# Local attention and two mixture layers on one core: copies ahead of exponentials on ScalarE, and one conversion operation on GpSimd

## The chip, the core and the metric

The kernel runs on one core of a Trainium2 chip. A core has five engines with queues of their own, each worked off in order: TensorE (PE in the rows, PEld for its weight loads), VectorE (DVE), ScalarE (ACT), GpSimd (POOL), and SyncE (SP), which here only starts transfers. They wait for each other through semaphores. The metric is the device time of one execution in microseconds (us). Lower is better.

## The reference

```
scores = scale * q @ k.T                    # 4 batches x 8 heads, 576 x 576, head width 64
mask   = (0 <= rel < 64), else -1e9         # each row looks back at most 63 positions
attn   = exp(scores - rowmax) / (rowsum + 1e-9);   x = attn @ v        # 2304 x 512
h = x @ w_in;  g = elu(h);  x = g @ w_out   # 512 -> 2048 -> 512
P = exp(x @ w_gate - max);  8 rounds of: divide rows by their sums, columns by theirs
out = sum over 8 experts e of  P[:, e] * (relu(x @ w1[e]) @ w2[e])     # 512 -> 1024 -> 512
```

The inputs q, k, v are 32-bit; `w_in` and `w_out` come as pairs of 32-bit words of 64-bit numbers.

## The kernel before

The program is one stream of calls in a fixed order, and each engine executes its own instructions in the order of these calls. Nothing is reordered at run time.

**Attention.** The 4 x 8 heads are 16 pairs of heads, each cut into three groups of 192 rows, so there are 48 groups, `n` = 0 to 47, group 0 to 2 for the first pair and so on. The loop `for m in range(NST + 3)` takes two groups a step through a pipeline of five stages, each a step apart. In step `m` the names are `nxt` (groups that are transposed), `new` (scores), `mid` (exponentials), `old` (probabilities transposed) and `fin` (multiplied by v):

- `pair_T` (L308, L314): four transposes on TensorE into `ptr`, then one ScalarE copy into `qkT`.
- `grp_S` (L340, L349): twelve score matmuls into `s`, then on VectorE three reductions, which add the mask, write `sp` and take the row's minimum into `smx`.
- `grp_E` (L366): three exponentials on ScalarE, in place on `sp`, with the row sums into `smx`.
- `grp_N` (L377, L378, L381): for both groups of a step, two short VectorE operations on `smx`, then on GpSimd one multiplication of `sp` for each group.
- `grp_P` (L389, L391): three transposes on TensorE into `pt`, then a ScalarE copy into `pT`.
- `v_shift` (L294): two GpSimd copies that build `ve`, the values shifted by 64 rows, once for each pair, in the step in which the pair's first group is in `old`.
- `grp_V` (L404) multiplies `pT` by `ve` and `vo`, and `grp_XH`, `grp_X` (L432, L439) write the result as a high part (ScalarE) and a low part (VectorE).

**Weights.** `f64_parts` turns a block of 64-bit weights into 32-bit ones, in six operations: L152 and L155 on VectorE (from the high words to `t`), L158 (the low words scaled, in place), L161 on ScalarE (magnitude of the high words), then L162 and L163 on VectorE, which join the parts. L179 and L180 on GpSimd (`w_split`) make a high and a low part from `t`. There are 32 blocks. The calls wait in a list `bg`, and `run_bg` takes two of them at three places of an attention step from step 1 on: ahead of `pair_T` and after each of the two halves of the step. A block takes eight calls (six operations, the next load, the split). Blocks 0 to 7 go through steps 1 to 11, two more are converted in steps 13 to 16. Blocks 10 to 15 run in the drain after the attention, the others in the middle stage.

**After that.** `slot` puts the matmuls of the first mixture layer between those of the attention, from step 9 on; before step 7 it puts a matmul on zeros (`warm`, L1170) there. After the last step the rest of the first part of that layer is drained; then come the other three parts of the layer (the middle stage), the gate, and the eight experts, which take most of the time.

Of the kernel before, what the change touches and what calls it, by code (L numbers as in the profile page):

```python
# [11 lines left out]
AF = mybir.ActivationFunctionType  # L12
ALU = mybir.AluOpType
# [5 lines left out]
def kernel(  # L19
# [14 lines left out]
    nc = tc.nc  # L34
# [13 lines left out]
    scale = 1.0 / float(D) ** 0.5  # L48
# [59 lines left out]
    def ps_ac(name):  # L108
        return ps.tile([P, 512], F32, tag="ac", bufs=4, name=name)
# [16 lines left out]
    def w_load(k):  # L126
        if k >= 2 * UF * NU:
            return
        u, i, m = w_at(k)
        f0 = (u * UF + i) * P  # L130
        t = raw_p.tile([P, 2 * DM], I32, tag="raw", bufs=NRAW, name="raw")
        if m == 0:
            nc.sync.dma_start(
                out=t.rearrange("p (c f) -> p c f", c=NCC),
                in_=w_in[:, 2 * f0:2 * (f0 + P)].rearrange("(c p) f -> p c f", p=P),
            )
        else:
            nc.sync.dma_start(out=t, in_=w_out[f0:f0 + P, :])
        raws[k] = t
# [3 lines left out]
    def f64_parts(src, t):  # L143

        w = src.rearrange("p (n two) -> p n two", two=2)
        lo, hi = w[:, :, 0], w[:, :, 1]
        ti = t.bitcast(I32)
        v = nc.vector  # L150
        return [
            lambda: v.tensor_scalar(  # L152
                ti, hi, 3, 0x3FFFFFF8, op0=ALU.logical_shift_left, op1=ALU.bitwise_and
            ),
            lambda: v.scalar_tensor_tensor(  # L155
                ti, hi, -0x40000000, ti, op0=ALU.bitwise_and, op1=ALU.bitwise_or
            ),
            lambda: nc.scalar.activation(  # L158
                lo, lo.bitcast(mybir.dt.uint32), AF.Copy, scale=2.0 ** -29
            ),  # L160
            lambda: nc.scalar.activation(hi.bitcast(F32), hi.bitcast(F32), AF.Abs),  # L161
            lambda: v.tensor_tensor(out=ti, in0=ti, in1=lo, op=ALU.add),  # L162
            lambda: v.scalar_tensor_tensor(  # L163
                t, hi.bitcast(F32), TINY, t, op0=ALU.is_ge, op1=ALU.mult
            ),
        ]
# [20 lines left out]
    def run_bg(n):  # L187
        for _ in range(min(n, len(bg))):
            bg.pop(0)()

    def w_tasks(k):
        def conv():
            bg[0:0] = w_conv(k) + [lambda: w_load(k + NRAW)]
            bg.pop(0)()

        return [conv, lambda: w_split(k)]
# [19 lines left out]
    def run_later():  # L216
        fs, later[:] = list(later), []
        for f in fs:
            f()
# [51 lines left out]
    def v_load(pi):  # L271
        b, hp = divmod(pi, NPAIR)
        h0 = 2 * hp

        vo = at.tile([P, 5, 2, D], F32, tag="vo", bufs=2, name="vo")
        for h in range(2):
            nc.sync.dma_start(
                out=vo[:, 0:4, h, :],
                in_=v[b, h0 + h, 0:512, :].rearrange("(w p) d -> p w d", p=P),
            )  # L280
        nc.sync.dma_start(
            out=vo[0:WIN, 4], in_=v[b, h0:h0 + 2, 512:S, :].rearrange("h p d -> p h d")
        )
        v_nat[pi] = (None, vo)
# [76 lines left out]
    def grp_E(n):  # L361
        sp, sm = g_st[n]
        g = n % NG
        for l in range(GRP):
            lo = WIN if g == 0 and l == 0 else 0
            nc.scalar.activation(  # L366
                sp[:, l, lo:],
                sp[:, l, lo:],
                AF.Exp,
                bias=sm[:, 0, l:l + 1],  # L370
                scale=-1.0,
                accum_out=sm[:, 1, l:l + 1],
            )

    def grp_N(ns):
        w = g_sm.pop(ns[0])[:, 1]
        nc.vector.tensor_scalar(w, w, 1e-9, None, op0=ALU.add)  # L377
        nc.vector.reciprocal(w, w)  # L378
        for i, n in enumerate(ns):
            sp, _ = g_st[n]  # L380
            nc.gpsimd.tensor_tensor(  # L381
                out=sp, in0=sp, in1=w[:, i].unsqueeze(2).to_broadcast([P, GRP, P]), op=ALU.mult
            )
# [10 lines left out]
    def grp_V(n, pv):  # L394
        pi, g = divmod(n, NG)
        b, hp = divmod(pi, NPAIR)
        pT = g_st.pop(n)
        ve, vo = v_nat[pi]
        for l in range(GRP):
            c = g * GRP + l  # L400
            vt, w = (vo, (c - 1) // 2) if c % 2 else (ve, c // 2)
            ks = slice(WIN, P) if c == 0 else slice(0, P)
            for h in range(2):
                nc.tensor.matmul(  # L404
                    pv[D * h:D * h + D, WIN * l:WIN * l + WIN],
                    vt[ks, w, h, :],
                    pT[ks, P * l + WIN * h:P * l + WIN * h + WIN],
                    start=True,
                    stop=True,
                )  # L410

    def grp_XH(ns, pv):
        segs = []
        for i, n in enumerate(ns):
            pi, g = divmod(n, NG)
            b, hp = divmod(pi, NPAIR)
            t0 = b * S + g * GRP * WIN
            t1 = t0 + GRP * WIN
            o = i * GRP * WIN
            while t0 < t1:  # L420
                j = t0 // TB
                n1 = min(t1, blocks[j][0] + blocks[j][1])
                x, z = t0 - blocks[j][0], n1 - blocks[j][0]
                if segs and segs[-1][:2] == [j, hp] and segs[-1][3] == x:
                    segs[-1][3] = z
                else:
                    segs.append([j, hp, x, z, o])
                o += z - x
                t0 = n1
        for j, hp, x, z, o in segs:  # L430
            src = pv[:, o:o + z - x]
            nc.scalar.activation(Xh[j][:, hp, x:z], src, AF.Copy)  # L432
            subs_x.append((j, hp, x, z, src))
# [3 lines left out]
    def grp_X():  # L437
        for j, hp, a, z, src in subs_x:
            nc.vector.tensor_tensor(  # L439
                out=Xl[j][:, hp, a:z], in0=src, in1=r(Xh[j][:, hp, a:z]), op=ALU.subtract  # L440
            )
        subs_x.clear()
# [703 lines left out]
    with tc.manual_schedule():  # L1146
# [43 lines left out]
        def ready():  # L1190
            if not avail:
                return False
            kind, _, x, h = avail[0]
            need = [(0, x, 0)] if kind == "i" else [(0, i, 1) for i in (2 * h, 2 * h + 1)]
            return all(w in wts for w in need)
# [14 lines left out]
        for m in range(NST + 3):  # L1210
            two = lambda x: [n for n in (2 * x, 2 * x + 1) if 0 <= n < NGRP]
            nxt, new, mid, old, fin = [two(m + 1 - x) for x in range(5)]
            if m == 0:
                for kk in range(NRAW):
                    w_load(kk)
            if ready():
                budget += 16.0 / per_b
            if fin:
                pv = ps_ac("pv")
                for i, n in enumerate(fin):  # L1220
                    grp_V(n, pv[:, i * GRP * WIN:(i + 1) * GRP * WIN])
                grp_XH(fin, pv)
            for n in new:
                grp_S(n)
            for n in mid[:1]:
                grp_E(n)
            for n in mid:
                if n and n % NG == 0:
                    v_load(n // NG)
            grp_X()  # L1230
            if fin and (m - 2) % per_b == 0:
                avail += subs[(m - 2) // per_b - 1]
            if m == 13:
                bg += [w_tasks(2 * UF + x)[0] for x in range(2)]
            rate = (2, 2, 2) if m else (0, 0, 0)
            run_bg(rate[0])
            slot(m, 2)
            for i in range(2):
                for n in nxt[i:i + 1]:
                    pair_T(n)  # L1240
                for n in old[i:i + 1]:
                    grp_P(n)
                for n in mid[1 - i:2 - 2 * i]:
                    grp_E(n)
                if i == 0:
                    for n in old:
                        if n % NG == 0:
                            v_shift(n // NG, 0)
                            v_shift(n // NG, 1)
                run_bg(rate[i + 1])  # L1250
                slot(m, 1 - i)
            if mid:
                grp_N(mid)
            run_later()
            for n in new:
                if n % NG == 0 and n // NG + 2 < B * NPAIR:
                    pair_load(n // NG + 2)
# [35 lines left out]
        for s, st in enumerate(steps):  # L1293
            u, j, i = st
# [50 lines left out]
        for u in range(1, 2 * KP):  # L1345
            n = 5 if 0 <= u - 2 < len(others) - N1 - N3 else 4
# [127 lines left out]
```

## Time and profile before

| what | value |
|---|---|
| median of 3 runs | 2026.53 us (2026.0 to 2027.12) |
| profiled execution, its own time | 2024.01 us |
| span of the profiled execution | 2022.2 us |
| TensorE busy | 1988.8 us (98%) |
| VectorE busy | 1412.7 us (70%) |
| ScalarE busy | 873.0 us (43%) |
| GpSimd busy | 772.4 us (38%) |
| mean granted TensorE clock | 0.995 |

The busy times are means over stages that differ. The 39 us of span in which TensorE has nothing lie mostly in the first 63 us and at the very end. A row of a profile names engine, line, output and inputs of an instruction, its start and its time in us; a trailing bracket gives the idle time of the engine ahead of it and what ended that.

### The profile page before, as it was taken

The numbers are of one execution on the slowest core, as the hardware profiler recorded it, in microseconds if no ns is written. First come the engines' busy times: TensorE is split into PE (matmuls) and PEld (weight loads), VectorE is DVE, ScalarE is ACT, GpSimd is POOL, SyncE is SP. The second block draws the span as 40 slices with busy tenths as digits, with TensorE's granted clock in tenths as the row PEclk, the third lists the DMA queues.
The fourth block names the chain that finished last, engine by engine and source line by source line (L and its number), as shares of the span: only waits on it lengthen the run. The fifth ranks groups of instructions, "written<-read, shape, count | busy, mean of one in ns | idle before, by whom it ended". The sixth has DMA issues, their size and how long they took to land.

```text
span 2022.2 us, 36406 instructions
## 1 busy us (share of the span) xinstructions
PE 1988.8 (98%) x13197; PEld 1849.8 (91%) x13197; DVE 1412.7 (70%) x2727; ACT 873.0 (43%) x1839; POOL 772.4 (38%) x753
## 2 busy tenths in 40 slices
PE   7999999999999999999999999999999999999998
PEld 6788888888878888889999999999999999999998
DVE  5754786858588665557777777777777777777776
ACT  6876455546443343333343333333334333333332
POOL 4533232324255555343353323233335333323332
PEclk9999999999999999999999999999999999999999
DMA  7540245438599999958878777777788877777774
GB/s 169 123 107 24 75 157 171 151 125 301 202 368 325 372 374 361 340 208 274 280 246 277 248 248 249 248 248 248 250 279 262 266 248 250 248 248 249 248 248 131
DMA packets 288628, 477.48 MB, mean 236 GB/s; under 512 B 78081, under 2 KB 144705, under 8 KB 284609
## 3 DMA queue, kind: packets, MB, share of 16 engines
q1 hardware_dynamic: 288368, 475.11, 71.7%
q8 instruction: 106, 1.74, 0.4%
q14 instruction: 74, 0.60, 0.1%
q10 hardware_dynamic: 80, 0.03, 0.0%
HBM read 348.14 MB, written 126.88 MB: 235 GB/s over the span
## 4 chain that ended last, share of the span: by engine, by line
PE 84%; DVE 5%; issue 4%; ACT 2%; DMA 2%; POOL 1%; SPq 1%; DVEq 0%; POOLq 0%; ACTq 0%
PE la L1043 15%; PE ob L1116 13%; PE oa L1116 13%; PE lb L1043 11%; PE ac L875 2%; PE ac L876 2%; PE ac L877 2%; PE p L857 2%; PE p L859 2%; PE p L858 2%; PE p L204 2%; PE p L205 2%; PE p L206 2%; PE ac L525 2%; PE ac L523 2%
## 5 line engine op out<-in xcount | busy, mean ns | idle before, releaser
L1025 POOL TENSOR_TENSOR h<-s,h 128x384 fp32r<-128x384 f32 x304 | 373.3, 1247 | 711.9 <-ACT h L1016 640.7
L1043 PE MATMUL la<-xf,w1f 128*128 128x384 f32 x1824 | 361.6, 336 | 6.5 <-ACT a L1056 4.8
L1043 PEld LDWEIGHTS la<-xf,w1f 128*128 128x128 f32 x1824 | 311.9, 189 | 8.7 <-ACT a L1056 5.2
L1116 PE MATMUL oa<-w2f,h 128*128 128x256 f32 x2394 | 307.3, 282 | 0.8 <-DVE acc L1137 0.8
L1116 PE MATMUL ob<-w2f,h 128*128 128x256 f32 x2394 | 307.3, 282 | 0.0
L1116 PEld LDWEIGHTS oa<-w2f,h 128*128 128x128 f32 x2394 | 302.0, 190 | 1.0 <-DVE acc L1137 1.0
L1116 PEld LDWEIGHTS ob<-w2f,h 128*128 128x128 f32 x2394 | 302.1, 190 | 0.0
L1021 DVE SCALAR_TENSOR_TENSOR h<-c,h 128x384 fp32r<-128x384 f32 x228 | 211.3, 927 | 120.0 <-ACT h L1016 119.9
L1043 PE MATMUL lb<-xf,w1f 128*128 128x384 f32 x1368 | 274.4, 335 | 0.0
L1043 PEld LDWEIGHTS lb<-xf,w1f 128*128 128x128 f32 x1368 | 237.5, 189 | 0.0
L1016 ACT ACTIVATE h<-s 128x384 fp32r<-128x384 f32 x304 | 154.7, 524 | 146.8 <-DVE s L1060 61.2
L1016 ACT ACTIVATE h<-c 128x384 fp32r<-128x384 f32 x228 | 119.1, 522 | 182.5 <-DVE c L1051 126.1
L1137 DVE SCALAR_TENSOR_TENSOR acc<-oa,Pr,acc 128x256 f32<-128x256 f32 x393 | 165.1, 474 | 42.2 <-PE oa L1116 42.2
L1137 DVE SCALAR_TENSOR_TENSOR acc<-ob,Pr,acc 128x256 f32<-128x256 f32 x381 | 160.1, 474 | 40.2 <-PE ob L1116 40.2
L696 POOL TENSOR_TENSOR sw<-rw 128x256 f32<-128x256 f32 x110 | 103.9, 944 | 214.6 <-DVE f L726 148.6
L1056 ACT ACTIVATE v<-la 128x384 f32<-128x384 f32 x76 | 37.4, 492 | 199.1 <-PE la L1043 199.0
L246 ACT ACTIVATE hh<-p 128x512 fp32r<-128x512 f32 (+1 forms) x80 | 39.2, 490 | 193.8 <-PE p L859 193.8
L857 PE MATMUL p<-xh,f 128*128 128x512 f32 (+1 forms) x320 | 108.7, 340 | 0.0
L859 PE MATMUL p<-xh,f 128*128 128x512 f32 (+1 forms) x320 | 107.7, 336 | 0.0
L858 PE MATMUL p<-xl,f 128*128 128x512 f32 (+1 forms) x320 | 107.6, 336 | 0.0
L1060 DVE SCALAR_TENSOR_TENSOR s<-c,s 128x384 f32<-128x384 f32 x152 | 103.0, 677 | 5.4
L247 DVE SCALAR_TENSOR_TENSOR hl<-p,hh 128x512 fp32r<-128x512 f32 (+1 forms) x80 | 44.2, 555 | 88.4 <-ACT hh L246 88.3
(155 smaller groups left out, 3694.4 us busy)
## 6 DMA issues: line engine op xcount, KB each, us to landing
w1f<-wdi SPq DMA_DIRECT2D x532, 256.0 KB, 3.7
w2f<-wdo SPq DMA_DIRECT2D x266, 512.0 KB, 3.8
wdo<-f SPq DMA_DIRECT2D x28, 1024.0 KB, 7.6
rw<-in_moe_w_dram SPq DMA_DIRECT2D x220, 128.0 KB, 4.5
wdi<-f SPq DMA_DIRECT2D x27, 1024.0 KB, 6.8
wdo<-f SPq DMA_DIRECT2D x28, 768.0 KB, 5.2
wdi<-f SPq DMA_DIRECT2D x27, 768.0 KB, 4.7
raw<-in_moe_w_in_dram SPq DMA_DIRECT2D x16, 512.0 KB, 4.0
```

The lines of the kernel that those rows point to most:

```text
L247: nc.vector.scalar_tensor_tensor(gl[:, :n], p1[:, :n], 0.0, r(gh[:, :n]), op0=ALU.max, op1=ALU.subtract)
L696: nc.gpsimd.tensor_tensor(out=sw[:, o], in0=a, in1=b, op=op)
L857: nc.tensor.matmul(p1[:, :n], w[:, s, 0, cs], xh, start=(c == 0), stop=False)
L858: nc.tensor.matmul(p1[:, :n], w[:, s, 0, cs], xl, start=False, stop=False)
L859: nc.tensor.matmul(p1[:, :n], w[:, s, 1, cs], xh, start=False, stop=(c == NCC - 1))
L1016: nc.scalar.activation(h[:, 0], src, AF.Relu if relu else AF.Copy)
L1021: nc.vector.scalar_tensor_tensor(h[:, 1], src, 0.0, r(h[:, 0]), op0=ALU.max, op1=ALU.subtract)
L1025: nc.gpsimd.tensor_tensor(out=h[:, 1], in0=src, in1=r(h[:, 0]), op=ALU.subtract)
L1043: nc.tensor.matmul(o, w[:, a, c, :], x[:, b, c, :], start=first and c == 0 and z == 0, stop=last and c == 1 and z == 2, skip_group_check=True,
L1060: nc.vector.scalar_tensor_tensor(d[nm], d[a], 0.0, d[b], op0=ALU.max, op1=op)
L1116: nc.tensor.matmul(o[:, c * HB2:(c + 1) * HB2], hs[p][:, a, c * P:(c + 1) * P], w[:, p, b, :], start=fresh and c != 1 and p == 0 and z == ...
L1137: nc.vector.scalar_tensor_tensor(a, src, pe, a, op0=ALU.mult, op1=ALU.add)
```

## The change

Two edits. In `f64_parts` the operation L158 goes from ScalarE to GpSimd. In the attention loop `grp_E` is called at the end of a step for the groups whose scores were made in this step, no longer in the next step in two halves; and `grp_N` for these groups is called in the next step right after `grp_S`, no longer at that step's end.

```
-            lambda: nc.scalar.activation(
-                lo, lo.bitcast(mybir.dt.uint32), AF.Copy, scale=2.0 ** -29
+            lambda: nc.gpsimd.tensor_scalar(
+                lo, lo.bitcast(mybir.dt.uint32), 2.0 ** -29, 0.0, op0=ALU.mult, op1=ALU.add
             ),
...
             for n in new:
                 grp_S(n)
-            for n in mid[:1]:
-                grp_E(n)
+            if mid:
+                grp_N(mid)
...
                 for n in old[i:i + 1]:
                     grp_P(n)
-                for n in mid[1 - i:2 - 2 * i]:
-                    grp_E(n)
...
                 run_bg(rate[i + 1])
                 slot(m, 1 - i)
-            if mid:
-                grp_N(mid)
+            for n in new:
+                grp_E(n)
```

The order of TensorE's and of SyncE's instructions is the same in both programs. GpSimd, before, over steps 5 to 7: the two L381 at the head of each step's piece are those of the step before, then come the step's clearing of `sp` (L332), split and `ve`.

```order
L294 TENSOR_SCALAR ve<-vo 64x640
L294 TENSOR_SCALAR ve<-vo 64x512
L381 TENSOR_TENSOR sp<-sp,smx 128x384 x2
L332 MEMSET sp 128x64
L179 TENSOR_SCALAR w0h<-t 128x512
L180 TENSOR_TENSOR w0l<-t,w0h 128x512
L294 TENSOR_SCALAR ve<-vo 64x640
L294 TENSOR_SCALAR ve<-vo 64x512
L381 TENSOR_TENSOR sp<-sp,smx 128x384 x2
```

GpSimd in the changed kernel, from step 5 to step 6:

```order
L381 TENSOR_TENSOR sp<-sp,smx 128x384 x2
L294 TENSOR_SCALAR ve<-vo 64x640
L294 TENSOR_SCALAR ve<-vo 64x512
L158 TENSOR_SCALAR raw<-raw 128x512
L332 MEMSET sp 128x64
L381 TENSOR_TENSOR sp<-sp,smx 128x384 x2
L179 TENSOR_SCALAR w0h<-t 128x512
L180 TENSOR_TENSOR w0l<-t,w0h 128x512
L294 TENSOR_SCALAR ve<-vo 64x640
L294 TENSOR_SCALAR ve<-vo 64x512
L158 TENSOR_SCALAR raw<-raw 128x512
```

The two L381 of a step now belong to the scores of the step before, as they did, but their two VectorE operations stand elsewhere. VectorE in step 2 of both programs, the end of the scores' reductions and what follows them:

```order
 L349 ISA sp,smx<-s,mask 128x128
 L349 ISA smx 128x1
+L377 TENSOR_SCALAR smx<-smx 128x6
+L378 RECIPROCAL smx<-smx 128x6
 L439 TENSOR_TENSOR xl_98<-pv,xh_93 128x384
 L162 ISA t<-raw,t 128x1024
```

L377 and L378 used to stand ahead of the first reduction of a step; now they stand behind its last one, and so do the L381 that wait for them. ScalarE in the changed kernel, over one step (step 4) and into the next:

```order
L314 ACTIVATE qkT<-ptr 128x2x192
L391 ACTIVATE pT<-pt 128x384
L161 ACTIVATE raw<-raw 128x512
L314 ACTIVATE qkT<-ptr 128x2x192
L391 ACTIVATE pT<-pt 128x384
L366 ACTIVATE sp,smx<-sp,smx 128x128 x6
L432 ACTIVATE xh_93<-pv 128x384
```

Before, three of the six L366 stood ahead of the first L314 of a step and three between the first L391 and the second L314, with an L158 ahead of each L161.

## Rows read from the trace of the kernel before

**Rows 1.** Busy time by engine in stretches; then granted clock, transfer share, GB/s.

```profile
23.70:63.20 39.50, 31.52 (x388) 25.89 (x388) 28.46 (x114) 31.04 (x116) 25.16 (x34) 0.90 0.67 149
63.20:210.00 146.80, 146.77 (x1346) 120.09 (x1347) 85.42 (x319) 107.69 (x351) 59.81 (x81) 0.99 0.32 78
210.00:230.00 20.00, 18.47 (x121) 16.62 (x120) 17.79 (x25) 8.36 (x14) 7.69 (x8) 1.00 0.40 131
230.00:420.00 190.00, 190.00 (x912) 160.39 (x912) 133.05 (x212) 100.34 (x180) 60.30 (x68) 1.00 0.42 142
```

**Rows 2.** Timeline, TensorE: the score matmuls of steps 3, 7, 8 and 9.

```profile
23.68 2.09 PE L340 MATMUL s<-qkT 64*64 64x64 f32 x24
...
51.03 1.43 PE L340 MATMUL s<-qkT 64*64 64x128 f32 x24
56.30 1.53 PE L340 MATMUL s<-qkT 64*64 64x128 f32 x24
63.11 2.44 PE L340 MATMUL s<-qkT 64*64 64x64 f32 x24
```

**Rows 3.** The chain that ended last, end of step 8: start, us, what.

```profile
58.92 0.84 POOL sp L381
...
59.84 1.15 POOL ve L294
...
62.05 1.12 PE pv L404 x16
```

**Rows 4.** Timeline, ScalarE: copies and exponentials, steps 1 and 3.

```profile
15.91 0.47 ACT L314 ACTIVATE qkT<-ptr 128x384 f32<-128x384 f32 x1
...
24.18 0.39 ACT L366 ACTIVATE sp<-sp,smx 128x128 f32<-128x128 f32 x1
...
24.56 0.39 ACT L366 ACTIVATE sp<-sp,smx 128x128 f32<-128x128 f32 x1
...
29.41 0.47 ACT L314 ACTIVATE qkT<-ptr 128x384 f32<-128x384 f32 x1
29.78 0.48 ACT L391 ACTIVATE pT<-pt 128x384 f32<-128x384 f32 x1
```

**Rows 5.** Timeline, GpSimd: steps 2 and 6.

```profile
21.59 1.41 POOL L294 TENSOR_SCALAR ve<-vo 64x640 f32<-64x640 f32 x2
...
44.03 1.61 POOL L381 TENSOR_TENSOR sp<-sp,smx 128x384 f32<-128x384 f32 x2 [3.55 <-DVE smx L378]
...
45.70 0.62 POOL L179 TENSOR_SCALAR w0h<-t 128x512 fp32r<-128x512 f32 x1
46.40 1.27 POOL L180 TENSOR_TENSOR w0l<-t,w0h 128x512 fp32r<-128x512 f32 x1
47.76 1.79 POOL L294 TENSOR_SCALAR ve<-vo 64x640 f32<-64x640 f32 x2
```

**Rows 6.** Timeline, VectorE: step 6, and the reductions of step 7.

```profile
46.90 1.06 DVE L152 TENSOR_SCALAR t<-raw 128x512 int32<-128x512 int32 x1
47.99 1.08 DVE L155 SCALAR_TENSOR_TENSOR t<-raw,t 128x512 int32<-128x512 int32 x1
49.52 0.17 DVE L377 TENSOR_SCALAR smx<-smx 128x6 f32<-128x6 f32 x1 [0.45 <-ACT sp L366]
...
53.04 0.29 DVE L349 CUSTOM_DVE_ANT_0 sp<-s,mask 128x128 f32<-128x128 f32 x1
```

**Rows 7.** Instructions on `raw`: ns min/median/max, first and last start.

```profile
L152 DVE TENSOR_SCALAR t<-raw x32: 412/421/1475, 13.2 to 401.4; 128x512 int32<-128x512 int32 x32
...
L158 ACT ACTIVATE raw<-raw x32: 637/663/683, 14.8 to 401.8; 128x512 int32<-128x512 uint32 x32
```

**Rows 8.** The chain in the drain: start, us, what.

```profile
211.27 1.48 DVE t L152
...
212.77 0.69 DVE t L155
...
221.26 1.49 DVE t L152
```

## The prediction

> **What bounds the kernel now.** I first read the busy times by stretch [rows 1]. From 63 to 210 us, and again from 230 to 420 us, TensorE is busy without a gap (146.77 of 146.80 us, 190.00 of 190.00). The order of its instructions doesn't change, so these stretches only shift. Time can be won or lost in two places. One is the start: from the scores of step 3 to those of step 9 [rows 2] TensorE is busy for 31.5 of 39.5 us. These are six steps, 63.11 - 23.68 = 39.43 us, or 6.6 us each. The other is the drain at 210 to 230 us, where it idles for 1.5 of 20 us.
>
> In the six steps I then read the chain that ended last. ScalarE is on it in most steps: copies and exponentials take turns with TensorE, and each step waits for its second `pT` copy. But at the end of step 8 the chain runs over GpSimd: the multiplications L381, then the two copies to `ve`, then TensorE [rows 3]. `grp_V` of step m + 1 needs the `ve` of step m at once, and that is a second bound close behind the first. Of the drain I read the chain too: there it runs over VectorE's conversions [rows 8] until TensorE, short of low parts, waits.
>
> **What the change does at the start.** From ScalarE it takes 32 L158 of 0.66 us [rows 7], of which three for every four early steps, and it lets ScalarE's exponentials run while TensorE does `grp_V` and scores. ScalarE's own sum in a step: copies stand 0.37 us apart, exponentials 0.38 [rows 4]. That is 4 x 0.37 + 6 x 0.38 = 3.8 us, with about 0.5 for the high part of the result and at most 0.7 for an L161 some 5.0 to 5.2 us. If nothing else bound, a step could fall from 6.6 to 5.2.
>
> What stands against it is the new order on GpSimd. L377 and L378 now come behind the reductions of the same step's scores, the two L381 behind them, and `ve` behind those. Before, they ran early in a step (44.03 in step 6, with the split and `ve` behind them [rows 5]).
>
> Count from the start of a step's scores. They start at 51.03 in step 7 [rows 2]; the last reduction starts at 53.04 and takes 0.2 to 0.3 [rows 6], so the reductions end at +2.2. L377 and L378, 0.2 each, and a handoff make 0.5 [rows 6], so the L381 start at +2.7 and, with 1.61 for two, end at +4.3. The `ve` copies take 1.41 undisturbed [rows 5]: +5.7. `grp_V` still has 0.3 to 0.7 us to do after `ve` (62.05 to the next scores is 1.1 with slower matmuls [rows 2, 3]): the next scores start at +6.2.
>
> - Steps 3 and 5, with a `ve`: 6.2 each. In step 5 the split of step 4 is still on GpSimd, because it waits for L163 behind the new L158: +0.5.
> - Step 6 has a split ahead of `ve`, 45.70 to 47.67, 2.0 us [rows 5]: 8.2, and 0.3 for reductions that stand behind L162, which now waits for a GpSimd L158 behind `ve`.
> - Step 8 has an L158 ahead of `ve`. Its price on GpSimd is not in the trace. The nearest row below is L179 (one input, same shape, 0.62), the nearest above L180 (two inputs, 1.27) [rows 5]. It has one input, so I take 0.7 and keep 0.6 and 1.3: 7.0.
> - Steps 4 and 7 have no `ve`: ScalarE's 5.2.
>
> The sum is 6.2 + 5.2 + 6.7 + 8.5 + 5.2 + 7.0 = 38.8 us against 39.4: -0.6. ScalarE's gain is used up by GpSimd.
>
> This sum has no collisions. In step 6 L152 took 1.06 us and L155 1.08 instead of 0.42 and 0.69, while GpSimd's L180 and `ve` ran, and `ve` took 1.79 instead of 1.41 [rows 5 to 8]. L152 ended 0.3 after L180: they took turns. In the changed order each step with a `ve` has two conversion operations of VectorE behind the low part of the result, at the time of the L381 and `ve`: L162 and L163 in steps 3 and 8, L152 and L155 in 5 and 6. If each holds GpSimd for its own length, a step's chain grows by 1.1 to 1.4 us, four steps by 5. So the six steps lie between -0.6 and +5; I take the middle, **+2.2**.
>
> The Trainium skill, "SBUF — State Buffer", section "Who interferes with whom", says that a VectorE instruction with two SBUF inputs, or in a mode with two ports, and a GpSimd instruction that reads SBUF exclude each other for a whole instruction. The collision of step 6 agrees. By that rule alone the six steps would stand at the upper end, +5; by the undisturbed durations at -0.6.
>
> Steps 0 to 2: the exponentials of groups 2 and 3 now come behind the second `qkT` copy of step 1 (15.91 [rows 4]), and on ScalarE that copy stands behind L161, which waits for L155. L155 now meets the L381 of groups 0 and 1, whose L377 and L378 stood behind L163 and now stand ahead of L152. So the copy comes at 15.9 (no collision) to 17.2. From there: six exponentials 2.3 with the copy's 0.4, L377 and L378 with handoff 0.5, two L381 1.6, split 2.0, `ve` 1.4, rest of `grp_V` 0.7, in all 8.9. The scores of step 3 start at 24.8 to 26.1, with two conversion operations in between at up to 27.5, against 23.68 [rows 2]: +1.1 to +3.8. I take **+2.4**.
>
> The granted clock is 0.90 over the six steps [rows 1]: after an idle stretch TensorE runs at the lower level for a while. It still idles ahead of several steps' scores, so I leave that as it is.
>
> **The drain and the middle stage.** In the drain the chain goes through VectorE. L152 or L155 of a block meets the split of the block before: L152 takes 421 ns at the median and 1475 at most [rows 7], and the chain holds two such L152 (211.27 and 221.26 [rows 8]) and, between them, a block whose L155 is the one that is held. On GpSimd the new L158 stands right behind that split, and L155 or L162 has to let it pass: 0.65 more for each of these three blocks, 2.0 us. It is 0 where L158 slips into a time in which VectorE reads PSUM, and 1.3 x 3 = 3.9 if L158 is as slow as L180. I take **+1.5**. Taking L158 from ScalarE gives nothing here: L161, behind it, waits for L155 anyway.
>
> In the middle stage 16 L158 cost VectorE up to 0.65 each, 10 us. It is busy 133 of 190 us and TensorE never waits [rows 1], so that cover holds it at nothing; without cover it would be these 10 us.
>
> **Sum.** 2.4 + 2.2 + 1.5 = +6.1 us. The terms come from an execution of 2024.01 us (span 2022.2 and 1.8 around it), 2.5 below the median of the runs; I add them to the median: 2026.5 + 6.1 = **2032.6 us**. With all terms at their ends: +0.5 and +12.7.
>
> **Rivals.**
> *ScalarE's pace.* If `ve` isn't held up, because the reductions end earlier or `grp_V` finds enough else to do, all six steps run at 5.2: 31.2 instead of 39.4, -8.2; with +1.1 at the start and +1.5 in the drain -5.6, or 2020.9 us. For it: ScalarE leads the chain in most steps now. Against it: `ve` bounds step 8 already with its L381 at +2.6 (58.92 against scores at 56.30 [rows 2, 3]) and the new order puts them at +2.7 in every step. It decides as soon as `ve` lies before +4.7.
> *A wash.* Durations as they stand, no collisions, L158 hidden in the drain: 1.1 - 0.6 + 0 = +0.5 us, up to +3 with one of the two dear: 2027 to 2029.5 us. For it: collisions are not the rule, since half of the L152 took 421 ns or less [rows 7].
> *VectorE becomes the bound in the middle stage.* There four L786 sit ahead of some L158, and L162 behind them would hold `gl`. VectorE is idle for 57 of 190 us and TensorE never waits [rows 1], so I give it little; it would add up to 10 us: 2042.6.
>
> **Chances.** Forecast 0.58, ScalarE's pace 0.16, wash 0.20, VectorE's bound 0.06. The range 2021 to 2040 leaves out about 0.16. A measurement of this kernel can tell about 0.2%, 4 us, from no change. Faster by more: 0.15, from the first rival. Within: the wash and the forecast's low end, 0.26. Slower: 0.59.
>
> **What would show it.** Right: scores of step 3 at 25 to 27 us, of step 9 at 65 to 70; TensorE's `pv` waiting for `ve` (GpSimd) in steps 3, 5, 6 and 8 and no longer for `pT`; longer L152 and L155 beside L158; a wait for `gl` of 2 to 4 us in the drain; no wait between 230 and 420 us. Wrong: step 9 before 63 us, or an L158 well above 1.3 us, which would add to step 8 and the drain and put the time above the range.

## The result, and the profile after

The changed kernel takes 2042.16 us (median of four runs, 2038.66 to 2044.29) against 2026.26 us of the kernel before (four runs, 2024.38 to 2027.12). The ratio is 1.0080 with an interval of 1.0065 to 1.0095, or 16.2 us more. The forecast was slower by 6.1 us, with a range up to 2040. The sign was right and the size was not.

| | before | after |
|---|---|---|
| profiled execution, its own time | 2024.01 us | 2042.18 us |
| span of it | 2022.2 us | 2040.4 us |
| scores of step 3 / step 9 | 23.68 / 63.11 | 26.88 / 73.80 |
| scores of step 14 | 101.89 | 116.93 |
| last matmul of the drain (L476) | 230.6 | 247.4 |
| last matmul of the middle stage (L523) | 542.7 | 559.3 |
| last expert matmul of the first kind (L875) | 879.6 | 897.6 |

By stretch, in the two profiled executions, against the terms of the prediction: steps 0 to 2 grew by 3.2 us (predicted 2.4); the six steps from 3 to 9 by 7.5 (2.2); steps 9 to 14 by 4.3 (0); from there to the end of the drain 1.8 (1.5); the middle stage -0.2 (0). The last 1.4 lie between the middle stage and L875, where nothing was touched; that stretch took 336.7 to 338.5 us in the eleven kernels traced here, in no order that follows an edit, so I count it as scatter between executions. The stretches add up to 18.0 of the 18.2 us between the two profiled spans; the 16.2 come from all runs, so the stretches need not add up to them.

Busy time by stretch of the kernel after (stretch, its length, busy time of PE, PEld, DVE, ACT and POOL with the count of instructions, granted clock, transfer share, GB/s):

```profile
26.88:73.80 46.92, 34.12 (x387) 27.85 (x385) 29.40 (x114) 29.49 (x112) 30.51 (x37) 0.86 0.56 123
73.80:117.00 43.20, 41.73 (x392) 34.31 (x392) 28.70 (x102) 29.79 (x101) 22.40 (x28) 0.90 0.43 106
117.00:226.00 109.00, 108.61 (x959) 88.44 (x960) 59.60 (x216) 71.34 (x232) 42.90 (x58) 1.00 0.28 64
...
246.80:436.60 189.80, 189.80 (x911) 160.17 (x910) 136.42 (x211) 92.12 (x164) 71.39 (x83) 1.00 0.43 142
```

Against [rows 1], which is finer here for steps 9 to 14 of the kernel before:

```profile
63.11:102.00 38.89, 38.88 (x392) 31.98 (x392) 26.91 (x102) 31.98 (x108) 18.23 (x26) 0.97 0.46 116
```

In the six steps TensorE idles for 46.92 - 34.12 = 12.8 us, before for 39.50 - 31.52 = 8.0; that is 4.8 more of waiting. The other 2.6 us are busy time: as many matmuls take longer, at a granted clock of 0.86 instead of 0.90. In steps 9 to 14 the same 392 matmuls take 41.73 us instead of 38.88, at 0.90 instead of 0.97, and there are 1.5 us of waiting, nearly all of it at the end of step 11. In the middle stage TensorE has still no gap.

TensorE's score matmuls [rows 2], and its waits ahead of `pv` (the bracket is the idle time and what ended it):

```profile
25.13 0.48 PE L404 MATMUL pv<-pT,ve 64*64 64x64 f32 x4 [3.75 <-POOL ve L294]
...
26.88 2.61 PE L340 MATMUL s<-qkT 64*64 64x64 f32 x24
...
46.96 0.33 PE L404 MATMUL pv<-pT,ve 64*64 64x64 f32 x4 [3.27 <-POOL ve L294]
...
48.62 2.61 PE L340 MATMUL s<-qkT 64*64 64x64 f32 x24
...
57.49 0.33 PE L404 MATMUL pv<-pT,ve 64*64 64x64 f32 x4 [3.41 <-POOL ve L294]
...
58.56 2.62 PE L340 MATMUL s<-qkT 64*64 64x128 f32 x24
...
64.18 1.53 PE L340 MATMUL s<-qkT 64*64 64x128 f32 x24
...
71.72 0.33 PE L404 MATMUL pv<-pT,ve 64*64 64x64 f32 x4 [3.63 <-POOL ve L294]
...
73.80 2.61 PE L340 MATMUL s<-qkT 64*64 64x64 f32 x24
...
97.92 0.33 PE L404 MATMUL pv<-pT,ve 64*64 64x64 f32 x4 [1.37 <-POOL ve L294]
...
99.23 2.61 PE L340 MATMUL s<-qkT 64*64 64x64 f32 x24
```

Each wait of over 3 us for `ve` is followed by scores that take 2.6 us instead of 1.43; so is the wait of 1.37 at the end of step 11. The waits of the first 440 us, summed by what ended them (us in total, times, longest):

```profile
PE pv L404 <- POOL ve L294: 16.1, 8, 3.7
PE p L477 <- DVE gl L235: 2.5, 2, 1.6
```

The kernel before had:

```profile
PE pv L404 <- ACT pT L391: 6.1, 5, 1.8
PE pv L404 <- POOL ve L294: 3.4, 3, 2.3
```

Now `pT` doesn't appear. The clock around the wait of step 8, in stretches of 2 us (columns as above):

```profile
68.00:70.00 2.00, 0.09 (x1) 0.00 (x0) 0.37 (x2) 2.00 (x9) 1.90 (x3) 1.00 1.16 247
70.00:72.00 2.00, 0.28 (x6) 0.21 (x6) 1.50 (x2) 0.98 (x6) 1.84 (x3) 0.98 1.09 190
72.00:74.00 2.00, 1.72 (x26) 1.42 (x26) 0.21 (x1) 0.09 (x1) 1.83 (x3) 0.50 0.37 47
74.00:76.00 2.00, 2.00 (x24) 2.00 (x22) 0.66 (x6) 0.40 (x1) 0.83 (x2) 0.50 0.54 217
76.00:78.00 2.00, 2.00 (x12) 1.67 (x10) 1.51 (x10) 0.52 (x2) 0.37 (x1) 0.50 0.01 2
```

TensorE has next to nothing to do from 68 to 72 us, and from 72 to 78 it works at 0.50, the lower of its two levels (1.2 of 2.4 GHz). The price of this wait is paid after it, mostly in step 9, which the prediction had put among the stretches that "only shift".

GpSimd and VectorE in step 5 [rows 5, 6], with L158 now on GpSimd:

```profile
37.64 1.62 POOL L381 TENSOR_TENSOR sp<-sp,smx 128x384 f32<-128x384 f32 x2 [0.50 <-DVE smx L378]
...
39.34 0.66 POOL L158 TENSOR_SCALAR raw<-raw 128x512 int32<-128x512 uint32 x1
...
40.03 0.69 DVE L162 CUSTOM_DVE_ANT_0 t<-raw,t 128x1024 uint16<-128x1024 uint16 x1 [1.97 <-POOL raw L158]
...
40.83 0.69 DVE L163 SCALAR_TENSOR_TENSOR t<-raw,t 128x512 f32<-128x512 f32 x1
...
41.44 0.28 DVE L349 CUSTOM_DVE_ANT_0 sp<-s,mask 128x128 f32<-128x128 f32 x1
...
42.31 1.27 POOL L180 TENSOR_TENSOR w0l<-t,w0h 128x512 fp32r<-128x512 f32 x1
...
42.70 0.91 DVE L377 TENSOR_SCALAR smx<-smx 128x6 f32<-128x6 f32 x1
...
43.98 1.79 POOL L381 TENSOR_TENSOR sp<-sp,smx 128x384 f32<-128x384 f32 x2 [0.40 <-DVE smx L378]
...
45.12 1.20 DVE L155 SCALAR_TENSOR_TENSOR t<-raw,t 128x512 int32<-128x512 int32 x1
...
45.86 1.74 POOL L294 TENSOR_SCALAR ve<-vo 64x640 f32<-64x640 f32 x2
```

The scores of this step start at 39.53. But VectorE stands at L162, which waits 1.97 us for L158, and that stands behind the L381 of the step before. So the first reduction comes at 41.44. Then L377, six columns and usually 0.17 us, takes 0.91 beside L180 and ends with it (43.61 and 43.58); L381 takes 1.79 instead of 1.61 and `ve` 1.74 instead of 1.41 beside L152 and L155. `ve` ends at 47.6, 8.1 us after the scores began. The two L381 themselves start 4.45 us after the scores here (43.98), and 3.8 us after them in steps 3, 6 and 8. In the kernel before, two L381 stand ahead of `ve` as well, but they start 0.6 us ahead of the scores in step 3 and 0.2, 0.1 and 1.8 us behind them in steps 5, 6 and 8.

The conversion's instructions [rows 7] (ns: least, median, most):

```profile
L152 DVE TENSOR_SCALAR t<-raw x32: 385/422/1501, 13.9 to 418.2; 128x512 int32<-128x512 int32 x32
L155 DVE SCALAR_TENSOR_TENSOR t<-raw,t x32: 691/1097/1670, 14.4 to 419.3; 128x512 int32<-128x512 int32 x32
...
L158 POOL TENSOR_SCALAR raw<-raw x32: 640/657/1007, 16.3 to 421.6; 128x512 int32<-128x512 uint32 x32
L162 DVE CUSTOM_DVE_ANT_0 t<-raw,t x32: 676/685/1177, 17.0 to 424.0; 128x1024 uint16<-128x1024 uint16 x32
```

L158 on GpSimd costs 0.66 us, as it did on ScalarE. In the drain [rows 8] the chain holds four long L155 in a row, of which the first two are shown; before, it held two long L152 and one long L155:

```profile
222.62 0.35 DVE t L152
...
222.99 1.67 DVE t L155
...
227.71 0.40 DVE t L152
...
228.12 1.66 DVE t L155
```

### The profile page after: what moved, and what is told of

Read it like the earlier page. It is cut to its first block, busy times and chain, and to the rows that moved or that the text cites. A ratio compares the mean times of both kernels' runs of the same rounds, so it can differ in the third digit from the quotient of the medians.

```text
span 2040.4 us, 36454 instructions
## 1 busy us (share of the span) xinstructions
PE 1999.0 (98%) x13197; PEld 1858.1 (91%) x13197; DVE 1419.6 (70%) x2727; ACT 857.7 (42%) x1807; POOL 800.6 (39%) x785
## 3 DMA queue, kind: packets, MB, share of 16 engines
q8 instruction: 106, 1.74, 0.3%
## 4 chain that ended last, share of the span: by engine, by line
PE 87%; DVE 5%; DMA 2%; ACT 2%; POOL 1%; issue 1%; SPq 1%; DVEq 0%; POOLq 0%; ACTq 0%
PE la L1043 15%; PE ob L1116 14%; PE oa L1116 13%; PE lb L1043 11%; PE ac L523 2%; PE p L204 2%; PE p L205 2%; PE p L206 2%; PE ac L524 2%; PE ac L525 2%; PE p L859 2%; PE p L857 2%; PE p L858 2%; PE ac L875 2%; PE ac L876 2%; PE ac L877 2%
```

## The experiments

Two theories were held against each other at first: that the new order of the calls makes the loss (`ve` behind the multiplications L381, and these behind the step's reductions; theory Q, for the queue), and that L158 on GpSimd does (theory L). Each kernel below was timed against the kernel before on the same chip, except the last, which ran once with a profile. A difference in us is the ratio's share of 2026.3 us; its interval is about 3 us to either side, 2 where a kernel ran ten times.

**The order alone (e1_reorder_only): the changed kernel with L158 back on ScalarE.**

```
-            lambda: nc.gpsimd.tensor_scalar(
-                lo, lo.bitcast(mybir.dt.uint32), 2.0 ** -29, 0.0, op0=ALU.mult, op1=ALU.add
+            lambda: nc.scalar.activation(
+                lo, lo.bitcast(mybir.dt.uint32), AF.Copy, scale=2.0 ** -29
```

> The reorder of exponentials and normalisation alone, L158 stays on ScalarE. Theory Q (the queue: the multiplications L381 now stand behind the scores' reductions and ahead of the copies to ve, which TensorE needs at once): most of the 16 us remain, +9 to +14 against the kernel before, TensorE waits 8 us or more for ve. Theory L (the operation moved to GpSimd, with its collisions on the port shared with VectorE, is the cause): 0 to +3.

Measured: 2036.52 us, ratio 1.0054 (1.0039 to 1.0069), 10.9 us more than before. `pv` waits for `ve` for 17.8 us in all, the six steps take 44.8 us. That is within what theory Q had, and far from the 0 to +3 of theory L.

**L158 alone (e2_l158_only): the order of before, L158 on GpSimd.** Shown against the changed kernel:

```
-            if mid:
-                grp_N(mid)
+            for n in mid[:1]:
+                grp_E(n)
...
+                for n in mid[1 - i:2 - 2 * i]:
+                    grp_E(n)
...
-            for n in new:
-                grp_E(n)
+            if mid:
+                grp_N(mid)
```

> L158 on GpSimd alone, exponentials and normalisation where they were before. Theory Q: +2 to +5, of which about 1.5 in the drain. Theory L: +12 to +16.

Measured: 2025.4 us over ten runs, ratio 1.0006 (0.9996 to 1.0015): nothing that can be told, +1.2 us by the ratio. That is less than the +2 to +5 expected, and theory L's +12 to +16 is out. Its wait for `gl` in the drain is 2.5 us, as in the changed kernel. So the order makes the loss. But the two parts don't add up: 10.9 and 1.2 make 12.1, and together they cost 16.2. In the order of the change, moving L158 costs 5.3 us, with an interval of some 4 to either side. Steps 5 and 8, where it stands ahead of reductions or of `ve`, take 9.09 and 9.62 us with it on GpSimd and 7.96 and 8.58 without.

**`ve` ahead of the multiplications (e3_ve_first): both parts of the change, and `v_shift` called ahead of `grp_N`.**

```
+            for n in old:
+                if n % NG == 0:
+                    v_shift(n // NG, 0)
+                    v_shift(n // NG, 1)
             if mid:
                 grp_N(mid)
...
-                if i == 0:
-                    for n in old:
-                        if n % NG == 0:
-                            v_shift(n // NG, 0)
-                            v_shift(n // NG, 1)
```

> The changed kernel with the two copies to ve called ahead of grp_N in a step; both edits are kept. Theory Q: TensorE's waits for ve (16.1 us in the changed kernel) fall below 4 us, the time falls to -5 to +4 against the kernel before. Theory L: nothing changes for the collisions, +11 to +16.

Measured: 2029.58 us over ten runs, ratio 1.0018 (1.0009 to 1.0028), 3.6 us more than before. Three quarters of the loss are gone, and the waits for `ve` fall from 16.1 to 1.1 us. That is within theory Q's range. What is left shows in two steps of the trace (whose execution, at 2024.77 us, is the fastest of the ten): step 5 takes 9.81 us, with two L381, L158, L162, L163, and only then the reductions, and step 9 takes 9.86 where the kernel before took 7.76. In each, VectorE's L162 stands waiting for an L158 behind two L381, 1.97 us in step 5 and 3.05 in step 9.

**The multiplications ahead of the reductions (e4_norm_first): both parts, and `grp_N` called ahead of `grp_S`.**

```
-            for n in new:
-                grp_S(n)
             if mid:
                 grp_N(mid)
+            for n in new:
+                grp_S(n)
```

> The changed kernel with grp_N called ahead of grp_S in a step, so that L377 and L378 stand ahead of the scores' reductions on VectorE again; ve stays behind L381. Theory Q: the multiplications start about 2.5 us earlier in a step and ve with them: -3 to +5 against the kernel before. If it is the mere presence of the multiplications ahead of ve and not the wait behind the reductions: +8 or more. Theory L: +11 to +16.

Measured: 2034.64 us, ratio 1.0045 (1.003 to 1.006), 9.1 us more. This gives back 7 of the 16 us; waits for `ve` are 10.2 us. That is the value that the expectation gave to the mere presence of L381 ahead of `ve`, but the run doesn't show that: the kernel before has them there too. In e4 they start 0.5, 3.1, 2.4 and 2.4 us after the scores in steps 3, 5, 6 and 8. This is earlier than in the changed kernel and still later than before; in part, L377 now waits for exponentials that stand at the end of the step ahead. So `ve` is late because the L381 ahead of it start late, and their place behind the reductions is one part of that.

**`ve` first, and L158 on ScalarE (e5_ve_first_l158_act): the edits of e1 and e3 together.**

> The two copies to ve ahead of grp_N, and L158 on ScalarE: the reorder without the edit to the conversion. Theory Q: nothing on GpSimd now holds VectorE's L162, so the reductions of step 5 aren't late as in e3; early steps at ScalarE's pace of 5 to 5.5 us, scores of step 9 at 55 to 60 us, -3 to -8 against the kernel before. Theory L (collisions alone matter): no better than e2, 0 to +2. If e3's loss has another source, +2 to +4 as in e3.

Measured: 2021.07 us over ten runs, ratio 0.998 (0.9971 to 0.999), 4.1 us less than the kernel before. This version beats both kernels, within the expected -3 to -8. Its waits of `pv`, of the first 440 us:

```profile
PE pv L404 <- ACT pT L391: 3.3, 5, 1.7
```

The wait for `pT` has gone from 6.1 us to 3.3, and `ve` stands at 0.7. The six steps take 37.22 us, 6.2 each and not the 5 to 5.5 of ScalarE's pace that the expectation named; the scores of step 9 start at 60.12. So there is a gain in this version once `ve` isn't held. How much of it comes from the exponentials' new place and how much from `ve` standing earlier than it did even before is not shown: no run put `ve` ahead in the old order, and both waits fell by about as much (2.8 and 2.7 us).

**The multiplications first, and L158 on ScalarE (e6_norm_first_l158_act): the edits of e1 and e4 together.**

> grp_N ahead of grp_S and L158 on ScalarE. Theory Q: L381 still stands ahead of ve, so TensorE still waits for ve, 5 to 10 us; +2 to +6 against the kernel before, less than e4's +9 by what the wait of L162 for L158 cost there. If the presence of L381 ahead of ve were harmless: 0 or below.

Measured: 2032.67 us, ratio 1.0038 (1.0025 to 1.0052), 7.7 us more than before, with 8.3 us of waits for `ve`. It is a little above the expected +2 to +6. In step 5, with the scores at 38.47, the trace has

```profile
40.20 0.21 DVE L377 TENSOR_SCALAR smx<-smx 128x6 f32<-128x6 f32 x1 [1.88 <-ACT sp L366]
...
40.79 1.62 POOL L381 TENSOR_TENSOR sp<-sp,smx 128x384 f32<-128x384 f32 x2 [0.40 <-DVE smx L378]
```

L381 start 2.3 us after the scores, where the kernel before has 0.2. So even with `grp_N` called first and without L158 on GpSimd, L381 come late, and `ve` behind them. What L158 costs differs between these pairs: e4 is 1.4 us above e6, which is within the noise, and e3 7.7 above e5.

**Five matmuls on zeros in the waits (e7_warm_in_wait).** The changed kernel with matmuls on zeros ahead of `grp_V` in the four steps that wait longest, to see what the lower clock costs.

```
+            if m in (3, 6, 7, 9):
+                warm(5)
             if fin:
                 pv = ps_ac("pv")
```

> The changed kernel with five more matmuls on zeros ahead of grp_V in steps 3, 6, 7 and 9, in which TensorE stands idle for ve; nothing else moves. If the lower clock after each idle stretch is a part of the loss: the score matmuls of these steps fall from 2.6 to 1.5 us, the granted clock of the early stretch rises above 0.9, and the time falls by 3 to 6 us to +10 to +13 against the kernel before. If the clock only shows the waits and costs nothing: unchanged, +15 to +17.

Measured: 2041.46 us, ratio 1.0082 (1.0068 to 1.0095), as the changed kernel. The four scores still took 2.10, 2.58, 2.15 and 2.61 us. Five matmuls did not keep the clock up, so neither of the two expected cases was tested, and the total says nothing on its price. In the profiled execution the early part is shorter than in the changed kernel all the same (the six steps 45.21 us at a clock of 0.88, steps 9 to 14 40.23 at 0.96), but from the end of the drain on it is 4.8 us longer, where nothing was touched. The stretch behind the last L875 took 1142.1 to 1146.3 us in the eleven kernels traced; such scatter can hide a gain of this size.

**Fourteen of them (e8_warm_full_wait).** The same with `warm(14)`, which fills the waits.

> As e7, but fourteen matmuls on zeros, about 3.2 us, which fill the idle time ahead of grp_V in steps 3, 6, 7 and 9 (3.3 to 3.8 us in the changed kernel). If the lower clock after the idle stretches is a part of the loss: the score matmuls of steps 3, 6, 7 and 9 take 1.5 us instead of 2.6, the clock stays at the upper level, +11 to +14 against the kernel before. If not: +15 to +18.

Measured: 2034.67 us, ratio 1.0043 (1.0027 to 1.006), 8.7 us more than before and 7.5 less than the changed kernel, which is below the expected +11 to +14. The scores of steps 6, 7 and 9 run at full clock:

```profile
47.42 1.43 PE L340 MATMUL s<-qkT 64*64 64x64 f32 x24
...
56.59 1.43 PE L340 MATMUL s<-qkT 64*64 64x128 f32 x24
...
70.28 1.43 PE L340 MATMUL s<-qkT 64*64 64x64 f32 x24
```

and around the wait of step 8 the stretches of 2 us read

```profile
68.00:70.00 2.00, 1.15 (x19) 0.72 (x20) 1.03 (x2) 0.00 (x0) 1.84 (x3) 1.00 0.51 83
70.00:72.00 2.00, 2.00 (x41) 1.76 (x37) 0.90 (x9) 0.49 (x1) 1.68 (x3) 1.00 0.73 236
```

The six steps take 44.1 us (2.8 less than in the changed kernel), steps 9 to 14 39.04 (4.1 less, and 0.3 from the 38.78 of before), and the scores of step 3 come 0.7 sooner, at 26.18. The sum, 7.6, agrees with the runs. Nothing else was changed, so the lower clock after these four waits, with the waits that it causes in turn, costs the changed kernel about 7.5 us. That is not the same as its share in the loss: the kernel before runs its six steps at 0.90 too, and no run filled its waits. What the two traces give directly is the longer busy time on as many matmuls, 2.6 us in the six steps and 2.85 in steps 9 to 14, 5.5 of the 16.2.

**No conversions before step 9 (e9_no_early_conversion).** The changed kernel with no conversion call in steps 1 to 8; they come later, and TensorE then runs short of weights, so only the six steps are read.

```
-            rate = (2, 2, 2) if m else (0, 0, 0)
+            rate = (2, 2, 2) if m > 8 else (0, 0, 0)
```

> The changed kernel without conversions of weights before step 9 (they run from step 9 on, so the matmuls of the first mixture layer come later and the whole time grows; only the stretch from the scores of step 3 to those of step 9 is of interest). If the turns that conversions take with L381 and ve are the part of the prediction that was too small: the six steps take 35 to 39 us instead of 46.9, TensorE's waits for ve fall to a half. If the order alone does it (L381 ahead of ve, whatever VectorE does): 44 us or more.

Measured once: 2070.2 us in all. The six steps, from 22.34 to 56.51 us, take 34.17 us at a clock of 1.00:

```profile
22.34:56.51 34.17, 27.78 (x389) 22.99 (x385) 12.58 (x96) 26.88 (x108) 15.62 (x24) 1.00 0.49 106
```

GpSimd's multiplications and `ve` have one length in all of them:

```profile
25.04 1.61 POOL L381 TENSOR_TENSOR sp<-sp,smx 128x384 f32<-128x384 f32 x2 [3.16 <-DVE smx L378]
26.74 1.41 POOL L294 TENSOR_SCALAR ve<-vo 64x640 f32<-64x640 f32 x2
```

This is just below the expected 35 to 39, and TensorE's waits for `ve` fall to a half as expected, to 5.8 us in the six steps from 10.8. So the new order by itself doesn't cost 46.9 us. It does so when conversions stand between its instructions. No run took the early conversions from the kernel before, so what the old order would take without them is not shown.

## Why the prediction was right about the sign and wrong about the size

The table has the length of each step from its scores to the next, in us: as the prediction counted it without collisions, and as the traces show it.

| step | counted | before | after | L158 on ACT (e1) | waits filled (e8) | no conversions (e9) |
|---|---|---|---|---|---|---|
| 3 | 6.2 | 7.37 | 8.10 | 8.13 | 7.84 | 6.13 |
| 4 | 5.2 | 6.14 | 4.55 | 4.55 | 4.54 | 4.56 |
| 5 | 6.7 | 6.71 | 9.09 | 7.96 | 8.86 | 6.61 |
| 6 | 8.5 | 7.13 | 9.94 | 9.86 | 9.17 | 6.13 |
| 7 | 5.2 | 5.27 | 5.62 | 5.72 | 4.17 | 4.13 |
| 8 | 7.0 | 6.81 | 9.62 | 8.58 | 9.52 | 6.61 |
| sum | 38.8 | 39.43 | 46.92 | 44.80 | 44.10 | 34.17 |

**The chain was right.** The prediction said that TensorE would wait for `ve` at the ends of steps 3, 5, 6 and 8 and no longer for `pT`. It does. (At the end of step 3 the trace names ScalarE for 1.03 us; that wait ended with the first of two `ve` copies that run from 32.87 to 34.67, and the chain that ended last goes through `ve` there.) The bare length of a step with a `ve`, 6.2 us by count, is 6.13 to 6.61 in e9. There the count holds link by link: L381 start 2.7 to 2.8 us after the scores (+2.7 in the prediction) and `ve` ends at 5.8 to 5.9 (+5.7). ScalarE's pace of 5.2 for a step without one was high: 4.1 to 4.6 in e9.

**The six steps, +2.2, were mis-sized: they measure +7.5.** Two things failed.

First, the start of L381, put at +2.7 with 0.5 and 0.3 us to spare in steps 5 and 6. In the changed kernel L381 start at +3.8, +4.5, +3.8 and +3.8 in steps 3, 5, 6 and 8, which is 5.2 us later in sum. The reductions ended 3.2 to 3.4 us after the scores began and not 2.2. In steps 3 and 6 the scores themselves took 2.6 us at the lower clock, 1.2 more each; in steps 5 and 8 L162, L163 or L152, L155 stood ahead of the reductions on VectorE, in step 5 waiting for L158. I had 0.5 in step 5 for that; e1 puts L158 alone at 1.1 there and 1.0 in step 8, where I had 0.7.

What the collisions added on GpSimd itself was not the part that was too small. I gave the six steps -0.6 without collisions and +5 with all, and took the middle, +2.2, which leaves 2.8 us for collisions. (By its own terms the upper end was +4.4, since the 5 us come on top of -0.6.) L381 takes 1.61 to 2.06 us in these four steps and `ve` 1.42 to 2.24, where e9 has 1.61 and 1.41 throughout: 2.4 us more in sum. VectorE's operations were held too: L155's median over all 32 rose from 694 to 1097 ns, that of L152 stayed (421 and 422). The Trainium skill, "SBUF — State Buffer", section "Who interferes with whom", lets a VectorE instruction with two SBUF inputs and a GpSimd instruction that reads SBUF shut each other out for a whole instruction. The trace agrees in kind: in the drain an L155, 0.69 us when alone, runs from 228.12 to 229.78 beside an L180 that ends at 229.24. By that rule alone the prediction had +5 for the six steps; their idle time grew by 4.8, but late starts are in that as well, so it is no test of the rule's size.

Second, "It still idles ahead of several steps' scores, so I leave that as it is" was said of the granted clock, which put the change of the clock at nothing. The waits became longer than those of before (3.3 to 3.75 us ahead of one `pv`, against 2.3 at most for `ve`), and the work behind them ran at 0.50. That is 2.6 us of busy time within the six steps, and part of the late starts above. With most of these waits filled (e8) the six steps are still 4.7 us longer than before.

**Steps 9 to 14, predicted at nothing, measure +4.3.** "These stretches only shift" holds for the order of the instructions and neither for their clock nor for the waits. TensorE's busy time grew by 2.85 us on the same 392 matmuls, and 1.5 us of waiting were added, 1.4 of it for `ve` at the end of step 11. By steps: step 9, behind the wait of step 8, is 1.3 us longer; step 11, with the new wait, 1.6; step 12, behind that wait, 1.5. In e8, with the wait of step 8 filled, these steps take 39.04 us in all.

**The start, +2.4, measures +3.2**, within its bounds of 1.1 to 3.8, with the scores of step 3 at 26.88 where 25 to 27 was named; those of step 9, named at 65 to 70, came at 73.80. **The drain, +1.5, measures +1.8**, with waits for `gl` of 2.5 us where 2 to 4 was named. Mostly L155 instead of L152 is now the one that is held. The wait for `gl` is 2.5 us in all six kernels that have L158 on GpSimd and the conversions in their place, 1.6 in the three others of the new order and 1.5 before: about 1.0 of the 1.8 us belongs to L158, the rest isn't placed. **The middle stage, 0**, has no wait; that rival is out. **L158's price, 0.7**, is 0.66.

**The rivals.** ScalarE's pace did not come. Once `ve` isn't held up, the time falls below that of before (e5, -4.1 us; the rival had -5.6), but not by the rival's mechanism: the six steps take 6.2 us each in e5 and 6.3 in e3, not 5.2, so that the nearness of -4.1 to -5.6 is luck. The wash is out; it would have needed the collisions to be the exception. What was missing among the rivals was the clock: no case had the longer waits lower it.

What stays open is how the late starts of steps 5 and 8 divide between VectorE's instructions that were held while they ran and those that only stood in the wrong order, and how much of the loss the clock makes against a kernel before that pays for it too. The rows show both kinds, and no run here took away one and left the other.

## What to carry to other kernels

When work moves on an engine that serves a waiting one, count from the waiting engine's side: the copy it needs first (`ve`) belongs ahead of the work it needs a step later (L381), and that alone turned +16.2 us into +3.6, or with L158 where it was into -4.1. The place in the queue is not all of it: the kernel before has L381 ahead of `ve` as well, but they started within 1.8 us of the scores and not 3.8 to 4.5 after them. A new or longer wait on TensorE has to be priced twice, once as idle time and once as the work behind it at the lower granted clock; here filling four waits gave back 7.5 us of 16.2, and part of that lay in a stretch that had no gap before. And two edits that are each harmless or bad alone can share a queue: L158 on GpSimd cost 1.2 us by its ratio in the old order, no more than can be told from nothing, and about 5 in the new one.

## What the runs showed of the hardware that I had not expected

- The profile gives a clock of 1.00 and 0.98 while TensorE stood nearly idle (0.37 us of work in 68 to 72 us) and 0.50 once work came back, for the 6 us from 72 to 78. The idle stretch itself looks harmless in the profile. The length of a wait alone doesn't tell what follows: behind 1.37 us at the end of step 11 the changed kernel's scores took 2.61 us, behind 1.50 at the same place those of e1 took 1.43, and in e9 the clock stayed at 1.00 over six steps with waits of up to 2.3 us.
- Five matmuls on zeros in a wait of over 3 us left the scores behind it at 2.1 to 2.6 us; fourteen brought three of four to 1.43. The one in step 3 still took 2.35.
- The kernel before pays for its clock too: its six steps hold 31.52 us of TensorE work, and the 389 matmuls of e9, at 1.00, take 27.78.
- A VectorE operation on six columns, 0.17 us as a rule, can last until the GpSimd instruction beside it ends: L377 took 0.91 us beside L180 and ended 0.03 us after it. It isn't new with the change: in the kernel before two of the 24 took 1.23 us, each beside an L180 of 1.58, and ended 0.03 us after it.
